# Row sums of two half-heads at once on 32 array columns, a later normalising multiply, and earlier loads, in a fused attention and gMLP block

## The chip, the cores and the metric

The kernel runs on one core of one Trainium2 chip. The metric is the device time of one execution in microseconds (us). Before: median 1973.52 us of 4 runs (1971.62 to 1976.08).

## The reference, cut to what matters

```python
h = _layernorm(x) * (1 + ca) + sa
x = x + ga * _A_ref(h, A_k_cache, A_v_cache, A_wq, A_wo)   # attention, 32 heads of 128, 2048 tokens
h = _layernorm(x) * (1 + cb) + sb
x = x + gb * _B_ref(h, B_w_in, B_w_sp, B_b_sp, B_w_out)    # gMLP, not touched by the change

# in _A_ref:
scores = einsum('bhqd,bhkd->bhqk', q, k_cache) * Dh ** -0.5
p = softmax(scores)                      # needs the sum of exp(scores) over the 2048 keys
o = einsum('bhqk,bhkd->bhqd', p, v_cache)
return o.transpose(...).reshape(B, Sq, H * Dh) @ wo
```

## The kernel before

Attention works in 64 half-heads `i` (32 heads, 1024 queries each) of 16 steps `kb` (128 keys each). A step makes scores (`sps`, two matmuls), takes the exponential on ScalarE (`pt`), multiplies by V (`ops`, two matmuls), and adds `pt` to a running sum `pacc` on VectorE. Queries of a later half (`qps`, 16 matmuls a half) are filled in between by the table `FILL`. At the end of a half, VectorE copies the two `ops` banks to `ou`.

`pacc` still has to be summed over its 128 partitions, inverted, and spread over all partitions:

```python
def bank_ps(...):  return psum.tile(..., tag="bank", bufs=3)   # two ops banks a half, three in all
def side_ps(...):  return psum.tile(..., tag="side", bufs=1)   # shared by qps and dps

def finish_den(i):
    dps = side_ps("dps", [P, 8])
    pv = state[i]["pacc"][:].rearrange("p (q c) -> p c q", c=8)
    for c_ in range(8):                      # weights: 128 columns of pacc; moving: ONE column of ones
        nc.tensor.matmul(dps[:, c_:c_ + 1], pv[:, c_, :], ones_bf[:, 0:1], start=True, stop=True)
    rec = small.tile([P, 8], FP32)
    nc.vector.reciprocal(out=rec[:], in_=dps[:])
    nc.sync.dma_start(rec_dram[i]..., rec[:])                  # 4 KB out
    rbc = att.tile([P, 1024], FP32, bufs=2)
    nc.sync.dma_start(rbc[:], rec_dram[i].partition_broadcast(P))   # 0.5 MB back, to all partitions
    state[i]["rbc"] = rbc

def normalise(i):
    oT = att.tile([P, 1024], BF16, bufs=2)
    nc.vector.tensor_mul(out=oT[:], in0=state[i]["ou"][:], in1=state[i]["rbc"][:])
    nc.sync.dma_start(oT_dram[h, :, ...], oT[:])
# ...
for g, (i, kb) in enumerate(steps):
    # ... exp, scores two steps ahead, fill, ops, pacc, ou ...
    if kb == 6 and i > 0:     finish_den(i - 1)
    elif kb == 12 and i > 0:  normalise(i - 1)

load_slab(0, outw)                     # oT of all heads for 256 tokens
attend_out(0, range(5)); finish_den(2 * H - 1); attend_out(0, range(5, H - 1)); normalise(2 * H - 1)
# ... then load_slab(1), load_slab(2), and for each tile ti of 128 tokens:
    xt = mid.tile([P, D], BF16, bufs=2); nc.sync.dma_start(xt[:], x_dram[:, ti, :])   # x_in
    attend_out(ti, ...)                # 64 acc matmuls
    # x1 = acc * ga + xt, layer norm -> hb; the next tile's TensorE work transposes hb (hps)
```

The softmax here doesn't subtract the row's maximum and nothing guards it: scores larger than these inputs give would overflow.

## Time and profile before

| | before |
|---|---|
| median | 1973.52 us |
| span of the profiled run | 1969.8 us |
| one half-head (from one `dps` to the next) | 17.99 us |
| its 80 matmuls of 512 columns, 0.2158 us each | 17.26 us |
| its 8 `dps` matmuls | 0.51 us |
| left over | about 0.2 us |

The page calls the TensorE (PE) 97% busy. The ends of pipelined matmuls are modelled there, so that share says little about what is lost; the chain of waits says more. It goes back from the last instruction to whatever released each step. Here is its summary by line for the middle of attention, 110 to 1240 us, in the kernel before:

```profile
by line: PE ops L279 39.2%; PE sps L209 38.4%; PE qps L190 19.1%; PE dps L233 2.8%; issue 0.2%; DVE pacc L289 0.1%; DVE oT L248 0.1%; DVE ou L285 0.1%; DVEq L289 0.0%; DVE qT L194 0.0%
```

`ops` and `sps` have the same number of matmuls of the same shape, and yet `ops` has 0.8% more of the chain, 9 us. The chain in order of time shows where they are (kernel before; columns: start in us, length in us, what):

```profile
604.32 0.43 PE qps L190 x2
604.75 0.22 PE ops L279
604.97 0.03 issue
605.00 0.38 PE ops L279
605.37 0.43 PE sps L209 x2
...
611.63 0.51 PE dps L233 x8
...
629.62 0.52 PE dps L233 x8
```

Two matmuls in a row take 0.43 us. At the start of a half the second `ops` takes 0.03 + 0.38 in place of 0.22: it had to be released, and in the records it starts 0.41 us after the matmul before it in place of 0.22. That is 0.19 us, once a half. What released it is on VectorE (DVE), in the timeline of the kernel before (start in us, length, instruction, idle time before it in brackets):

```profile
601.12 0.69 DVE L194 CAST qT<-qps 128x512 bf16<-128x512 f32 x1 [1.27 <-PE qps L190]
601.73 1.22 DVE L248 TENSOR_TENSOR oT<-ou,rbc 128x1024 bf16<-128x1024 f32 x1
602.86 1.48 DVE L289 TENSOR_TENSOR pacc<-pacc,pt 128x1024 bf16<-128x1024 bf16 x2
604.26 0.68 DVE L285 COPY ou<-ops 128x512 f32<-128x512 f32 x1
```

The `ou` copy frees the bank and ends at 604.94, just ahead of the matmul at 605.00. This is no accident of one half: the records have 61 such late `ops` matmuls, each 52 to 54 ns after the end of an `ou` copy. The copy is late because the multiply `oT` runs just before it. Finally, the waits at the transition from attention to the next stage (kernel before, 1235 to 1300 us; columns: total us, times, longest us):

```profile
DVE x L358 <- DMA x_in<-in_A_x_dram: 10.3, 1, 10.3
...
PE hps L144 <- DVE hb L139: 3.6, 1, 3.6
```

The load of `x_in` is queued behind 4 MB of slabs, VectorE waits for it, and the TensorE then stands 3.6 us.

### The profile page before, as it was taken

How to read it: one execution, taken by the hardware profiler on the slowest of the kernel's cores; microseconds unless marked ns; L12 is line 12 of the kernel's file. 1: busy time of each engine (PE TensorE's matmuls, PEld its weight loads, DVE VectorE, ACT ScalarE, POOL GpSimd, SP SyncE). 2: the span in 40 equal slices, each digit the busy share in tenths (PEclk: the TensorE clock that was granted, in tenths of full speed). 3: DMA queues.
4: the chain of work that ended last, by engine and by line, in shares of the span. 5: the costliest groups of instructions: out<-in, count | busy, mean ns of one | idle time of the engine just before them, and what ended most of it. 6: DMA issues, size and time to landing. Idle time of an engine off the chain costs nothing.

```text
span 1969.8 us, 24541 instructions
## 1 busy us (share of the span) xinstructions
PE 1905.1 (97%) x9313; PEld 886.1 (45%) x9313; DVE 1223.4 (62%) x1969; ACT 1105.7 (56%) x1149; POOL 27.0 (1%) x54
## 2 busy tenths in 40 slices
PE   5399999999999999999999999999999999999999
PEld 2244444444444444444444444444445544444444
DVE  4977777777777777777777777454446500233334
ACT  0089889898988898889888988300003333000000
POOL 0100000000000000000000000000000000000000
PEclk9599999999999999999999999999999999999999
DMA  9313222323323324234334322645215010223102
GB/s 318 87 42 88 77 80 81 92 70 86 82 70 90 89 60 109 70 112 124 106 93 127 88 78 58 167 136 171 82 43 124 1 32 22 75 49 91 37 7 75
DMA packets 279399, 171.74 MB, mean 87 GB/s; under 512 B 193648, under 2 KB 245872, under 8 KB 279280
## 3 DMA queue, kind: packets, MB, share of 16 engines
q1 hardware_dynamic: 279280, 170.16, 31.4%
q8 instruction: 73, 1.20, 0.3%
q14 instruction: 46, 0.38, 0.1%
HBM read 120.06 MB, written 24.90 MB: 74 GB/s over the span
## 4 chain that ended last, share of the span: by engine, by line
PE 94%; DMA 2%; DVE 2%; SPq 1%; POOL 0%; issue 0%; ACT 0%; POOLq 0%; DVEq 0%
PE ops L279 23%; PE sps L209 22%; PE qps L190 11%; PE acc L322 10%; PE gps L425 10%; PE zps L375 5%; PE bo L446 5%; PE zps L409 5%; PE dps L233 2%; DMA wm<-in_w_mod_dram 1%; SPq L308 1%; DMA xt<-in_A_x_dram 1%; PE mod_ps L110 1%; DVE stats L134 1%; PE hps L144 0%; DVE h1T L145 0%
## 5 line engine op out<-in xcount | busy, mean ns | idle before, releaser
L268 ACT ACTIVATE pt<-sps 128x1024 bf16<-128x1024 f32 x1024 | 1033.1, 1024 | 211.0 <-PE sps L209 179.7
L289 DVE TENSOR_TENSOR pacc<-pacc,pt 128x1024 bf16<-128x1024 bf16 x896 | 615.7, 687 | 125.8 <-ACT pt L268 78.4
L279 PE MATMUL ops<-pt,v_sb 128*128 128x512 bf16 x2048 | 618.8, 379 | 2.7 <-DVE ou L285 0.6
L209 PE MATMUL sps<-qT,kT 128*128 128x512 bf16 x2048 | 608.7, 379 | 0.8 <-DVE qT L194 0.6
L190 PE MATMUL qps<-h1T,wq_t 128*128 128x512 bf16 x1024 | 357.6, 382 | 3.4 <-DVE qT L194 2.2
L279 PEld LDWEIGHTS <-v_sb 128*128 128x128 bf16 x2048 | 199.9, 98 | 242.6 <-issue 0.8
L209 PEld LDWEIGHTS <-kT 128*128 128x128 bf16 x2048 | 197.4, 98 | 240.7 <-issue 22.3
L322 PE MATMUL acc<-wo_t,ot 128*128 128x512 bf16 x992 | 216.9, 379 | 0.3 <-DMA ot<-oT_dram 0.3
L377 ACT ACTIVATE z<-zps 128x448 bf16<-128x448 f32 x64 | 34.8, 544 | 294.8 <-PE zps L375 291.9
L425 PE MATMUL gps<-wsp,z 128*128 128x512 bf16 x896 | 193.9, 379 | 0.0
L428 DVE TENSOR_TENSOR g<-gps,b_bc 128x512 bf16<-128x512 f32 x56 | 38.8, 692 | 222.1 <-PE gps L425 222.1
L194 DVE CAST qT<-qps 128x512 bf16<-128x512 f32 x128 | 88.5, 691 | 135.4 <-PE qps L190 135.4
L190 PEld LDWEIGHTS <-wq_t 128*128 128x128 bf16 x1024 | 100.8, 99 | 125.4 <-issue 6.4
L322 PEld LDWEIGHTS <-ot 128*128 128x128 bf16 x992 | 96.3, 98 | 114.1 <-DMA ot<-oT_dram 0.8
L425 PEld LDWEIGHTS <-z 128*128 128x128 bf16 x896 | 87.7, 98 | 105.7
L375 PE MATMUL zps<-z2w,h2T 128*128 128x448 bf16 x512 | 97.3, 352 | 0.0
L446 PE MATMUL bo<-w_out_t,z1T 128*128 128x512 bf16 x448 | 97.2, 379 | 0.0
L409 PE MATMUL zps<-h2T,z1w 128*128 128x512 bf16 x448 | 96.9, 379 | 0.0
L248 DVE TENSOR_TENSOR oT<-ou,rbc 128x1024 bf16<-128x1024 f32 x62 | 75.4, 1215 | 0.0
L375 PEld LDWEIGHTS <-h2T 128*128 128x128 bf16 x512 | 50.0, 98 | 46.5 <-issue 0.2
L411 ACT ACTIVATE z1T<-zps 128x512 bf16<-128x512 f32 x56 | 33.4, 597 | 63.3 <-PE zps L409 63.3
L446 PEld LDWEIGHTS <-z1T 128*128 128x128 bf16 x448 | 43.9, 98 | 52.8
(59 smaller groups left out, 708.9 us busy)
## 6 DMA issues: line engine op xcount, KB each, us to landing
rbc<-rec_dram SPq DMA_DIRECT2D x64, 512.0 KB, 3.6
v_sb<-in_A_v_cache_dram SPq DMA_DIRECT2D x32, 512.0 KB, 4.7
oT_dram<-oT SPq DMA_DIRECT2D x62, 256.0 KB, 2.3
wm<-in_w_mod_dram SPq DMA_DIRECT2D x12, 1024.0 KB, 7.1
ot<-oT_dram SPq DMA_DIRECT2D x24, 512.0 KB, 6.7
wq_t<-in_A_wq_dram SPq DMA_DIRECT2D x8, 1024.0 KB, 8.3
wo_t<-in_A_wo_dram SPq DMA_DIRECT2D x8, 1024.0 KB, 5.7
xt<-in_A_x_dram SPq DMA_DIRECT2D x16, 256.0 KB, 2.7
```

What stands on the lines that cost most here:

```text
L190: nc.tensor.matmul(box["ps"][:], wq_t[:, dc, hc:hc + DH], h1T[:, dc, q0:q0 + 512], start=(dc == 0), stop=(dc == KD - 1))
L194: nc.vector.tensor_copy(out=out_t[:, j * 512:(j + 1) * 512], in_=box["ps"][:])
L209: nc.tensor.matmul(sps[:, j * 512:(j + 1) * 512], kts[h][:, kb * P:(kb + 1) * P], qts[(h, qh)][:, j * 512:(j + 1) * 512], start=True, stop ...
L248: nc.vector.tensor_mul(out=oT[:], in0=state[i]["ou"][:], in1=state[i]["rbc"][:])
L268: nc.scalar.activation(pt[:], s_tiles.pop(g)[:], ACT.Exp, scale=SCALE)
L279: nc.tensor.matmul(o_ps[j][:], vs[h][:, kb, :], pt[:, j * 512:(j + 1) * 512], start=(kb == 0), stop=(kb == NKB - 1))
L289: nc.vector.tensor_add(out=pacc[:], in0=pacc[:], in1=pt[:])
L322: nc.tensor.matmul(accs[ti][:, sl], lhs, wo_t[:, hh, sl], start=(hh == 0), stop=(hh == H - 1))
L375: nc.tensor.matmul(zps[:], h2T[:, dc, ti * P:(ti + 1) * P], z2w[:, dc, sl], start=(dc == 0), stop=(dc == KD - 1))
L409: nc.tensor.matmul(zps[:], w[:, dc, :], h2T[:, dc, q * 512:(q + 1) * 512], start=(dc == 0), stop=(dc == KD - 1))
L425: nc.tensor.matmul(gps[:], z2[s][:, f * P:(f + 1) * P], wsps[q][:, s, :], start=(s == 0), stop=(s == NT - 1))
L446: nc.tensor.matmul(bo[:], z1T[:, f, ti * P:(ti + 1) * P], w_out_t[:, f, sl], start=(f == 0), stop=(f == NF - 1))
```

## The change

Its intent: fewer and better shaped row-sum matmuls (a stationary block of 32 columns of ones, `pacc` moving, four groups of 32 array columns, two half-heads at once); the multiply at a place where VectorE is not needed for `ou`; loads at the transition ahead of need.

```diff
-    ones_bf = consts.tile([P, 1], BF16)
+    ones_bf = consts.tile([P, 32], BF16)
@@ def finish_den(i):
-        dps = side_ps("dps", [P, 8])
-        ... eight matmuls of one moving column, reciprocal, one write, one broadcast load (above)
+        # row sums of steps i and i + 1 at once
+        dps = side_ps("dps", [P, 512])
+        for k in range(2):
+            pacc = state[i + k]["pacc"]
+            for b in range(4):
+                nc.tensor.matmul(dps[32 * b:32 * b + 32, 256 * k:256 * k + 256],
+                                 ones_bf[:, :], pacc[:, 256 * b:256 * b + 256],
+                                 start=True, stop=True)
+        den = att.tile([P, 16, 32], FP32, name="den", tag="den")
+        nc.vector.transpose(den[:].rearrange("p c r -> p (c r)"), dps[:])
+        rec = small.tile([P, 32], FP32, name="rec", tag="rec")
+        nc.vector.memset(rec[:], 0.0)
+        nc.vector.reciprocal(out=rec[:, 0:16], in_=den[:, :, 0])
+        turned = small.tile([P, 32], FP32, name="turned", tag="turned")
+        nc.vector.transpose(turned[:], rec[:])
+        for b in range(4):
+            nc.sync.dma_start(rec_dram[i:i + 2]...[b], turned[32 * b:32 * b + 16, :])
+        rbc = att.tile([P, 2, 1024], FP32, name="rbc", tag="rbc", bufs=1)
+        nc.sync.dma_start(rbc[:], rec_dram[i:i + 2].partition_broadcast(P))
+        ... each of the two halves gets its part of rbc
@@ buffers: oT 2 -> 1, pacc 2 -> 3, ou 2 -> 3; load_slab and attend_out defined before the loop
+        if i == len(halves) - 1 and kb == 4:
+            load_slab(0, outw)
@@ in the loop
-        if kb == 6 and i > 0:
-            finish_den(i - 1)
-        elif kb == 12 and i > 0:
-            normalise(i - 1)
+        if kb == 6 and i > 0 and i % 2 == 0:
+            finish_den(i - 2)
+        elif kb == 3 and i > 2:
+            normalise(i - 3)
+        elif kb == 9 and i == len(halves) - 1:
+            normalise(i - 2)
@@ after the loop
-    finish_den(2 * H - 1)
+    finish_den(2 * H - 2)
     attend_out(0, range(5, H - 1))
+    normalise(2 * H - 2)
     normalise(2 * H - 1)
@@ next stage: x_in with 3 buffers, two tiles ahead, the first two issued before the slabs
+    load_x(0)
+    load_x(1)
     load_slab(1, mid)
...
-        xt = mid.tile([P, D], BF16, name="x_in", tag="x_in", bufs=2)
-        nc.sync.dma_start(xt[:], x_dram[:, ti, :])
+        if ti + 2 < NT:
+            load_x(ti + 2)
```

## The prediction

> **What bounds it now.** The TensorE. In the chain of waits, from 110 to 1240 us (attention), 39.2% are the `ops` matmuls, 38.4% `sps`, 19.1% `qps`, 2.8% `dps`. One half-head repeats every 17.99 us (`dps` to `dps`, 611.63 to 629.62). Its 80 matmuls of 512 columns at 0.2158 us (0.43 for two in the chain) need 17.26. The remaining 0.73 us is 0.51 us of eight `dps` matmuls (row sums, 64 ns each for one moving column) and about 0.2 us once a half: at 604.97 the chain has 0.03 us of issue and then one `ops` matmul of 0.38 instead of 0.22. The timeline shows why: this second `ops` bank becomes free with the `ou` copy, VectorE 604.26 to 604.94. VectorE was late because `oT` (1.22 us) ran at 601.73, just before the half ends.
>
> **What the change does, per pair of halves.**
> - Row sums: 16 single-column matmuls (2 x 0.51 = 1.02 us, all on the chain) become 8 of 256 columns, each on 32 array columns. One after another they would take 8 x 0.108 = 0.86 us (estimate from 0.2158 for 512) plus switching. The Trainium skill, "TensorEngine Tiling (Array Packing)", Key Properties, says that different tiles run matmuls in parallel and that changing the mode drains the TensorE; no trace yet shows either. If four run together, two rounds take about 0.22 us; with weight loads and two drains I estimate 0.6 us for the eight. Saved: 0.4 us a pair.
> - VectorE: 2 x 0.21 us of reciprocals become two transposes, a memset and a reciprocal, about 1.1 us (the large one estimated at 0.69 like the 512-element f32 copies). VectorE has room. But the side bank now stays taken until the large transpose ends; the next `qps` matmul uses it 0.86 us later (the four matmuls in between). That is nearly a tie; I allow 0.15 us a pair of new wait.
> - `oT` moves from step 12 to step 3. The `ou` copy can then start when the last `ops` ends, and the 0.2 us a half should go: 64 x 0.19 = 12 us. At step 3 VectorE has 0.88 us idle before the next cast, so 1.13 us more fits nearly.
> - Transition: `x_in` and the first slab load earlier. Now VectorE waits 10.27 us for `x_in` behind the slab loads and TensorE stands 3.6 us (waits: PE `hps` for `hb`). This goes. Against it, the tail chain of the last row sums grows (about 1.4 us on VectorE instead of 0.2, four writes, 1 MB broadcast instead of 0.5) to about 11.5 us, and 52 `acc` matmuls (11.2 us) cover it: perhaps 0.5 to 1 us of wait.
>
> **Sum.** 32 x (0.42 - 0.15) = 8.6; plus 12; plus 3.6 - 0.8: about 23 us. Stages before 100 us and after 1300 us do not change. Predicted 1950 us, 8 in 10 from 1935 to 1965. Faster by over 2%: 0.09; within 2%: 0.90; slower: 0.01.
>
> **What would show it.** The half-head period: from 17.99 us to a pair of about 35.3 (2 x 17.26 + 0.75). No 0.38 us `ops` piece at a half's start. The `dps` piece of a pair: 0.6 us if tiles run together, 1.0 or more if not. `qps` waiting for VectorE's `den` after row sums: 0 to 0.15 us. No `x_in` wait near the transition.
>
> **What would make it wrong.** Column tiles that run one after another with expensive drains (then about 10 us gain only); a 32-bit transpose at half speed, which would stall `qps` by 0.6 us a pair; tiles so cheap (0.3 us) that the gain nears 35 us; a slow tail.

## The result, and the profile after

| | before | after |
|---|---|---|
| median | 1973.41 us (13 runs) | 1936.74 us (8 runs, 1935.81 to 1936.99) |
| ratio | | 0.9812, 95% interval 0.9803 to 0.9822 |
| span of the profiled run | 1969.8 us | 1935.0 us |
| two half-heads | 35.98 us | 34.98 us |

A ratio is the mean time of one kernel's fast runs over that of the other's fast runs of the same rounds, so it is not quite the ratio of the medians. The gain is 36.7 us, 1.9%. It lies inside the range predicted, close to its lower end; the mean forecast was 23 us.

The chain of waits of the kernel after, by line, for the middle of attention (110 to 1200 us):

```profile
by line: PE sps L209 39.8%; PE ops L314 39.5%; PE qps L190 19.8%; PE dps L234 0.9%
```

`ops` no longer exceeds `sps`, and the row sums fell from 2.8% to 0.9%. In order of time, with the `dps` of the next pair (kernel after, chain):

```profile
592.01 0.43 PE qps L190 x2
592.45 0.43 PE ops L314 x2
592.88 0.43 PE sps L209 x2
...
598.71 0.43 PE ops L314 x2
599.14 0.33 PE dps L234 x8
599.47 0.54 PE sps L209 x2
600.01 0.43 PE ops L314 x2
600.44 0.23 PE qps L190
...
634.12 0.33 PE dps L234 x8
```

At the start of the half (592.45) two `ops` take 0.43 us: the 0.38 piece is gone. All eight `dps` matmuls take 0.33 us, and the `sps` pair behind them 0.54, which is 0.11 more than any other pair. So a pair of halves pays 0.44 us for its row sums. Before it paid 0.51 twice, and 0.02 twice in an `sps` pair of 0.45 behind them: 1.06 us. VectorE of the kernel after, timeline:

```profile
589.42 1.48 DVE L324 TENSOR_TENSOR pacc<-pacc,pt 128x1024 bf16<-128x1024 bf16 x2
591.40 0.69 DVE L320 COPY ou<-ops 128x512 f32<-128x512 f32 x1 [0.50 <-PE ops L314]
...
595.40 1.22 DVE L259 TENSOR_TENSOR oT<-ou,rbc 128x1024 bf16<-128x1024 f32 x1
596.54 1.48 DVE L324 TENSOR_TENSOR pacc<-pacc,pt 128x1024 bf16<-128x1024 bf16 x2
598.31 0.69 DVE L194 CAST qT<-qps 128x512 bf16<-128x512 f32 x1 [0.29 <-PE qps L190]
598.92 0.68 DVE L324 TENSOR_TENSOR pacc<-pacc,pt 128x1024 bf16<-128x1024 bf16 x1
599.52 0.72 DVE L238 STREAM_TRANSPOSE den<-dps 128x512 f32<-128x512 f32 x1
```

The `ou` copy now waits for the TensorE (0.50 us idle before it) and no longer the other way round. The `oT` multiply at step 3 still leaves 0.29 us before the cast. The transpose ends about 600.24. The `qps` matmul that wants its bank comes right after it, as the timeline of the TensorE shows (kernel after; the chain lays its pieces end to end, so its 600.44 is not the time at which this matmul started):

```profile
599.84 0.59 PE L314 MATMUL ops<-pt,v_sb 128*128 128x512 bf16 x2
600.29 0.38 PE L190 MATMUL qps<-h1T,wq_t 128*128 128x512 bf16 x1
```

In the records this `qps` starts 52 to 53 ns after the end of the transpose in every pair of the loop, the same distance as between the `ou` copy and the `ops` matmul above. So it is released by the transpose. It starts about 232 ns after the matmul before it, where 216 are usual: a wait of 0.016 us a pair. At the transition (1200 to 1265 us) no wait for `x_in` and no `hps` wait is left in the list of waits, and the chain there is TensorE work with only one gap, 1.2 us for the last exponential. The table of the period accounts for the gain: 1.00 us a pair, 32 pairs, 32 us; the transition gives about 4. (The two profiled spans differ by 34.8 us and not by 36.7: the profiled run of before was the fastest of its 13.)

### The profile page after: what moved, and what is told of

The parts are those of the page before. It is cut to its first block, busy times and chain, and to the rows that moved or that the text cites. A ratio compares the mean times of both kernels' runs of the same rounds, so it can differ in the third digit from the quotient of the medians.

```text
span 1935.0 us, 24004 instructions
## 1 busy us (share of the span) xinstructions
PE 1876.4 (97%) x9057; PEld 856.5 (44%) x9057; DVE 1251.3 (65%) x2033; ACT 1102.1 (57%) x1149; POOL 27.0 (1%) x54
## 4 chain that ended last, share of the span: by engine, by line
PE 96%; DVE 2%; DMA 2%; POOL 0%; ACT 0%; issue 0%; SPq 0%; POOLq 0%
PE sps L209 23%; PE ops L314 23%; PE qps L190 12%; PE acc L285 11%; PE gps L448 10%; PE zps L398 5%; PE bo L469 5%; PE zps L432 5%; DMA wm<-in_w_mod_dram 1%; DMA xt<-in_A_x_dram 1%; PE mod_ps L110 1%; PE dps L234 1%; PE hps L144 0%; DVE stats L134 0%; DVE h1T L145 0%; DVE h L138 0%
## 5 line engine op out<-in xcount | busy, mean ns | idle before, releaser
L314 PE MATMUL ops<-pt,v_sb 128*128 128x512 bf16 x2048 | 609.0, 379 | 0.3 <-ACT pt L303 0.3
L400 ACT ACTIVATE z<-zps 128x448 bf16<-128x448 f32 x64 | 34.8, 544 | 290.5 <-PE zps L398 287.6
L145 DVE COPY h2T<-hps 128x1024 bf16<-128x1024 bf16 x16 | 11.1, 691 | 98.7 <-PE hps L144 98.7
```

The source lines that it names most:

```text
L314: nc.tensor.matmul(o_ps[j][:], vs[h][:, kb, :], pt[:, j * 512:(j + 1) * 512], start=(kb == 0), stop=(kb == NKB - 1))
```

## The experiments

Each ran with five rounds. "More than after" means against 1936.7 us, the median of after both times it was timed (1936.74 and 1936.71). Medians of before in the three sets of rounds were 1974.94, 1973.99 and 1975.98 us.

### 1. `move_only`: the kernel before, with only the multiply moved

```diff
-            ou = att.tile([P, 1024], FP32, name="ou", tag="ou", bufs=2)
+            ou = att.tile([P, 1024], FP32, name="ou", tag="ou", bufs=3)
...
-        elif kb == 12 and i > 0:
+        elif kb == 3 and i > 1:
+            normalise(i - 2)
+        elif kb == 12 and i == len(halves) - 1:
             normalise(i - 1)
```

> The kernel before, with only the normalising multiply moved from step 12 of the next half to step 3 of the half after that (one more buffer for its input). Theory: the gain has three parts that add up, and this is one: the ou copy is no longer late, the 0.38 us ops piece at each start of a half turns into 0.22, so 64 x 0.19 = 12 us less, about 1961 us, and the half-head period in the trace falls from 17.99 to about 17.78 us. Rival: VectorE is only 62% busy and not the bottleneck, so moving its work gives nothing (1973 us) and the whole gain of the change is TensorE work taken away.

Measured: 1963.05 us against 1974.94, ratio 0.9941 (0.9929 to 0.9954), so 11.9 us less. The period in the chain is 17.80 us (606.88 to 624.68). The theory's 12 us hold; the rival, by which an engine at 62% cannot matter, falls. An average says nothing about who is late at one instant of each half.

### 2. `early_only`: the kernel before, with only the early loads

```diff
+        if i == len(halves) - 1 and kb == 4:
+            load_slab(0, outw)
...
+    load_x(0)
+    load_x(1)
     load_slab(1, mid)
...
-        xt = mid.tile(..., bufs=2); nc.sync.dma_start(xt[:], x_dram[:, ti, :])
+        if ti + 2 < NT:
+            load_x(ti + 2)
```

> The kernel before, with only the loads at the transition moved earlier: the first slab inside the last half, x_in two tiles ahead and in front of the slabs. Theory: the 3.6 us wait of hps for hb and the 0.35 us wait for the first slab go, 3 to 4 us less, about 1969.5 us. Rival: the slabs are then later and a new wait of the same size appears among the acc matmuls (no change, 1973 us).

Measured: 1968.98 us, ratio 0.9972 (0.9960 to 0.9985), which is 3 to 8 us less than before (6.0 by the medians). The profiled spans differ by 3.0 us (1966.8 against 1969.8). No new wait appeared.

### 3. `old_sums`: the kernel after, with single-column row sums

```diff
-        dps = side_ps("dps", [P, 512]) ... (eight matmuls, transpose, memset, reciprocal, transpose, four writes)
+        dps = side_ps("dps", [P, 16])
+        for k in range(2):
+            pv = state[i + k]["pacc"][:].rearrange("p (q c) -> p c q", c=8)
+            for c_ in range(8):
+                nc.tensor.matmul(dps[:, 8 * k + c_:8 * k + c_ + 1], pv[:, c_, :],
+                                 ones_bf[:, 0:1], start=True, stop=True)
+        rec = small.tile([P, 2, 8], FP32, name="rec", tag="rec")
+        nc.vector.reciprocal(out=rec[:]..., in_=dps[:])
+        nc.sync.dma_start(rec_dram[i:i + 2]..., rec[:])
```

> The kernel after, with the row sums made by 16 single-column matmuls for the two halves again, nothing else changed. Theory: each pair pays 1.02 us again instead of the 0.44 us that the chain after shows (0.33 dps, 0.11 longer sps), so 32 x 0.58 = 18.6 us more than after, about 1955 us. Rival (the whole gain is the row sums): back to about 1970 us.

Measured: 1955.45 us, 18.7 us more than after. Its chain has 1.00 us for sixteen `dps`. The matmuls alone are worth half of the gain, and not all of it.

### 4. `late_norm`: the kernel after, with the multiply at step 12 again

```diff
-        elif kb == 3 and i > 2:
-            normalise(i - 3)
-        elif kb == 9 and i == len(halves) - 1:
+        elif kb == 12 and i > 1:
             normalise(i - 2)
```

> The kernel after, with the normalising multiply back at step 12, everything else kept. Theory: the ou copy is late again, the second ops matmul of a half takes 0.38 us in the chain, 64 x 0.19 = 12 us more than after, about 1949 us. Rival: no change against after (1937 us).

Measured: 2027.69 us (one run of four at 2034.95), 91 us more than after and 53 us more than before. Both expectations missed by far. The list of waits of `late_norm` names it (total us, times, longest us):

```profile
PE ops L314 <- DVE ou L320: 70.0, 31, 3.7
DVE oT L259 <- DMA rbc<-rec_dram: 65.2, 31, 3.6
```

Both happen 31 times, once a pair. The chain of `late_norm` in one pair:

```profile
598.81 0.64 DVE den L238
...
601.94 1.62 DMA rec_dram<-turned
...
603.71 4.55 DMA rbc<-rec_dram
...
608.36 0.06 DVE oT L259
608.42 1.08 issue
609.50 0.69 DVE pacc L324
...
610.98 0.61 DVE ou L320
611.59 0.04 issue
611.64 0.38 PE ops L314
```

For two halves at once, the way from the row sums to the broadcast is long: 0.72 us for the large transpose (before: one reciprocal of 0.21), four writes issued one after another, and a load of 1 MB that took 4.55 us here where the load of 0.5 MB took 3.6 before. It is 9.5 us from 598.73, the start of `den`, to the landing at 608.26. Step 12 comes sooner than that. In the timeline of `late_norm` VectorE stands idle for 1.92 us in front of `oT` and does the `pacc` additions and the `ou` copy, which come behind it in the program, only after it; the TensorE waits for the bank (the 70.0 us above).

### 5. `half_late`: one of the two multiplies at step 12, with its data there

```diff
-        elif kb == 3 and i > 2:
+        elif kb == (12 if i % 2 and i < len(halves) - 1 else 3) and i > 2:
             normalise(i - 3)
```

> The kernel after, with the normalising multiply of every even half moved from step 3 to step 12 of the same later half, so that its broadcast has long landed; the other half's stays at step 3. late_norm lost 91 us, where 12 were forecast, because the multiply at step 12 stood waiting for the 1 MB broadcast and VectorE with it. Theory: with the data there, only the late ou copy remains: 31 halves x 0.19 = 6 us more than after (about 1943 us), and a 0.38 us ops piece at the start of every second half. Rival: the step-12 place is bad by itself, then some 40 us more (about 1978 us).

Measured: 1942.05 us, 5.3 us more than after. The expectation counted 31 halves; the edit moves 30 (odd `i` from 3 to 61), and the records have exactly 30 late `ops` matmuls, each 54 to 55 ns after the end of an `ou` copy. The chain shows the late piece in every second half only, 35.18 us apart:

```profile
594.27 0.03 issue
594.30 0.38 PE ops L314
600.94 0.33 PE dps L234 x8
629.45 0.03 issue
629.48 0.38 PE ops L314
```

So step 12 costs 0.18 us by its place (5.3 over 30), some 11 us if both halves of each pair pay it. The other 80 us of `late_norm` are left for the data not being there, which is how its list of waits has it (70.0 us of TensorE waits behind `ou`, 65.2 us of VectorE waits for `rbc`).

### 6. `one_group`: all eight row-sum matmuls on the same 32 array columns

```diff
-                nc.tensor.matmul(dps[32 * b:32 * b + 32, 256 * k:256 * k + 256],
+                nc.tensor.matmul(dps[0:32, 256 * k:256 * k + 256],
...
-        nc.vector.transpose(den[:]..., dps[:])
+        nc.vector.transpose(den[0:32]..., dps[0:32, :])        # den is set to 1 once
```

> The kernel after, with all eight row-sum matmuls of a pair sent to the same 32 array columns (the result is wrong on purpose; the unwritten part of den is set once). Theory: the 0.33 us of after comes from four column groups working at once; in one group the eight run one after another, 8 x 0.108 = 0.86 us, so 32 x 0.53 = 17 us more than after, about 1954 us. Rival: 256-column matmuls with 32 columns of weights are cheap by themselves: no change, 1937 us.

Measured: 1956.91 us, 20.2 us more than after. (Its output is wrong, which doesn't matter for the time. The comparison with the reference still passed, so a passed comparison is weak evidence for the row sums here.) The chain of `one_group`:

```profile
607.40 0.98 PE dps L237 x8
608.38 0.54 PE sps L209 x2
```

The records put the starts of the eight matmuls 109 to 120 ns apart (1, 120, 230, 339, 448, 557, 666, 775). In the kernel after they start at 1, 5, 8, 11 and again at 120, 125, 128, 130 ns: four at a time, in two rounds. That the groups work together is shown. The expectation was 17 us because it counted 0.86 us of streaming against all of the 0.33. In both kernels the next `sps` weight load starts 201 ns after the last row-sum start, so only the first 0.13 us of the 0.33 grew, to 0.78: 0.65 x 32 = 20.8 us.

### 7. `group_by_group`: the two loops exchanged

```diff
-        for k in range(2):
-            pacc = state[i + k]["pacc"]
-            for b in range(4):
+        for b in range(4):
+            for k in range(2):
+                pacc = state[i + k]["pacc"]
```

> The kernel after, with the two loops of the row sums exchanged: both matmuls of one column group in a row, then the next group. Result right. Theory: matmuls start in program order, so the second of a group holds up the next group; five rounds of 0.107 us instead of two, about 0.65 us instead of 0.33, and 32 x 0.32 = 10 us more than after, about 1947 us. Rival: groups are queued independently and the order does not matter: 1937 us.

Measured: 1937.61 us, 0.9 us more than after. The theory fell. In the chain the eight take 0.34 us. In the records they start at 2, 9, 15, 22 and then at 122, 129, 135, 142 ns. In program order the second matmul belongs to the same group as the first, and `one_group` shows that such a pair starts 109 ns apart or more. Four starts within 20 ns can therefore only be in four different groups: later groups went ahead of the waiting second matmul of the first. The spacing says the same: these starts are 6 to 7 ns apart, where in the kernel after, which changes the group with every matmul, they are 3 to 4 ns apart. This is inferred from the times; the records do not name the group. The extra 0.9 us is small and the two ranges do not overlap in the rounds of `after` (1937.42 to 1937.71 against 1935.81 to 1936.99), but they do in those of `after_again` (up to 1937.61); the chain has 0.01 us more in `dps` and 0.01 more in the `qps` behind it. The Trainium skill, "TensorE: Matmul & The Clock Gate", Part 3, "The mechanism", says that matmuls are "strict FIFO, no reordering". By this measurement that does not hold across column groups.

### 8. `four_wide`: four matmuls of 512 columns for eight of 256

```diff
-            for b in range(4):
-                nc.tensor.matmul(dps[32 * b:32 * b + 32, 256 * k:256 * k + 256],
-                                 ones_bf[:, :], pacc[:, 256 * b:256 * b + 256],
+            for j in range(2):
+                b = 2 * k + j
+                nc.tensor.matmul(dps[32 * b:32 * b + 32, :],
+                                 ones_bf[:, :], pacc[:, 512 * j:512 * j + 512],
```

> The kernel after, with four row-sum matmuls of 512 columns per pair in place of eight of 256, each column group still streaming 512 columns. Result right. Theory: 0.22 us of streaming and a fixed cost of switching on either side stay, so the two chain pieces together stay near 0.44 us; 0 to 2 us less than after, about 1936 us. Rival: the cost goes with the number of matmuls and weight loads, 0.055 us each: 0.22 us less a pair, 7 us less, about 1930 us.

Measured: 1936.13 us (1935.56 to 1936.84), 0.6 us less than after, and the two ranges overlap. The chain has 0.33 and 0.54 us, the same as after. The cost does not go with the number of matmuls and weight loads. This version is simpler, but it is not shown to be faster.

### 9. `after_again`: the kernel after, for the rounds of the next two

> The kernel after once more, on the same chip as the next two, to have its ratio in the same rounds: 1936 to 1938 us.

Measured: 1936.71 us, ratio 0.9804 (0.9790 to 0.9817). Against 0.9812 above, this shows how well two sets of rounds agree.

### 10. `no_early`: the kernel after, without the early loads

```diff
-        if i == len(halves) - 1 and kb == 4:
-            load_slab(0, outw)
+    load_slab(0, outw)                       # after the loop
...
-    load_x(0)
-    load_x(1)
...
-        if ti + 2 < NT:
-            load_x(ti + 2)
+        xt = mid.tile(..., bufs=2); nc.sync.dma_start(xt[:], x_dram[:, ti, :])
```

> The kernel after, with the loads at the transition put back to where they were before (first slab after the last half, x_in behind the slabs, two buffers). Theory: parts add up, so the wait of hps for hb returns, 3.5 to 5.5 us more than after (about 1941 us). Rival: the parts overlap and taking one away costs less than 1.5 us.

Measured: 1949.10 us, 12.4 us more than after: a miss, where the same loads give 3 to 8 us in `early_only`. The timeline of `no_early` (TensorE lines, idle time in brackets):

```profile
1219.67 3.91 PE L285 MATMUL acc<-wo_t,ot 128*128 128x512 bf16 x10 [1.49 <-DMA ot<-oT_dram]
...
1256.48 1.04 PE L144 MATMUL hps<-identity,hb 128*128 128x128 bf16 x8 [6.94 <-DVE hb L139]
1257.31 15.48 PE L285 MATMUL acc<-wo_t,ot 128*128 128x512 bf16 x62
```

and its busy time, granted clock and DMA share by stretch (the number before the DMA share is the clock):

```profile
1218.00:1222.00 4.00, 2.52 (x8) 0.92 (x8) 2.31 (x4) 1.04 (x2) 0.00 (x0) 0.78 1.19 305
1222.00:1226.00 4.00, 4.00 (x22) 1.44 (x21) 1.23 (x4) 0.00 (x0) 0.00 (x0) 0.79 0.51 123
...
1256.00:1260.00 4.00, 3.52 (x15) 1.87 (x16) 2.83 (x5) 0.00 (x0) 0.00 (x0) 0.50 0.01 2
```

The tail of the last pair is longer than that of one half, so the slabs start later and `x_in` behind them later still; the `hps` wait is 6.94 us where it was 3.6. In addition the clock fell. The 0.78 and 0.79 are means: the trace's record of the clock has 0.50 from 1220.25 for 3.41 us, and again from 1254.38 for 6.83 us, and 1.00 between. The ten `acc` matmuls after the first wait took 3.91 us where after needs 2.3 (1.6 us lost), and the `hps` and `acc` pieces after the second took 1.04 + 15.71 us in the chain where after has 0.45 + 13.81 (2.5 us lost). With the two waits, 1.49 and 6.94, this makes 12.5 us, about the 12.9 by which the profiled spans differ. The Trainium skill, "TensorE: Matmul & The Clock Gate", Part 1, says that the clock halves after an idle window of about 3.4 us, which is free-running. The wait of 6.94 us agrees. So does the 3.6 us wait in the kernel before, after which the clock stayed at 1.00: counted in steps of 3.413 us from the last change of the clock in that trace (97.82), a window ends at 1278.83, in the middle of the wait (1277.1 to 1280.7), so that neither window was idle throughout. The fall at 1220.25 does not agree: in the 3.41 us before it the TensorE was idle for 1.8 us only (waits of 0.32 and 1.49), much as in those two windows of the kernel before (1.7 and 1.9 us).

### 11. `extra_visit`: one more visit to the 32-column mode

```diff
+        if kb == 13 and i > 0 and i % 2 == 0:
+            idle = side_ps("idle", [P, 64])
+            for b in range(4):
+                nc.tensor.matmul(idle[32 * b:32 * b + 32, :], ones_bf[:, :],
+                                 h1T[:, 0, 0:64], start=True, stop=True)
```

> The kernel after, with one more visit of the TensorE to the 32-column mode in every second half, at step 13: four matmuls of 64 columns whose result nobody reads. Theory: of the 0.44 us a pair of after, 0.22 is streaming and about 0.2 is a fixed cost of going into the mode and out of it (0.09 us in front, 0.1 us behind), so each visit costs about 0.22 us, 31 x 0.22 = 7 us more than after. Rival: there is no fixed cost and the four small matmuls cost their streaming alone, 0.03 us, so 1 us more.

Measured: 1944.37 us, 7.7 us more than after, so 0.25 us for each of the 31 visits. Its chain:

```profile
610.78 0.14 PE idle L343 x4
610.92 0.54 PE sps L209 x2
```

0.14 plus the 0.11 of the longer `sps` pair is 0.25 us for 64 columns of streaming, which alone would be 0.03 us. So a visit has a fixed cost of about 0.22 us, and the rival falls. The Trainium skill, "TensorEngine Tiling (Array Packing)", Key Properties, says that a change of tiling mode drains the TensorE; this run fits that and gives the size of a whole visit. That the drain makes up all of the fixed 0.22 us is not shown.

No run beat after by more than the spread of its runs. The one that came nearest is `four_wide`.

## Why the prediction was right or wrong

**Right: what bounds the kernel, and the `ou` copy.** The prediction read 0.19 us a half from the chain and named the multiply as its cause; it forecast 12 us. `move_only` gave 11.9 us, and `half_late`, which puts back about half of it, cost 5.3. The 0.38 us piece went, as said. The multiply fitted at step 3: 0.29 us stayed idle before the cast.

**Right in kind, mis-sized: the row sums.** "with weight loads and two drains I estimate 0.6 us for the eight. Saved: 0.4 us a pair." They cost 0.33 + 0.11 = 0.44 us, and what they replaced cost 1.06, so 0.62 us a pair was saved: 20 us over 32 pairs where 13 were forecast. `old_sums` puts it at 18.7. Both halves of the estimate were right in kind. `one_group` shows that four groups run together, and `extra_visit` and `four_wide` show that the rest is a fixed cost of the visit. Only the size of that fixed cost, 0.22 us, was below what I allowed (0.38, the 0.6 less 0.22 of streaming). The prediction had named this case under what would make it wrong: "tiles so cheap (0.3 us) that the gain nears 35 us".

**Right in kind, mis-sized: the new wait for the side bank.** "That is nearly a tie; I allow 0.15 us a pair of new wait." It is a tie: the transpose releases the `qps` matmul in every pair, but the wait is 0.016 us, 0.5 us in all. The estimate put 0.86 us between the row sums and that `qps`; in the chain it is 0.97 (0.54 + 0.43). This term was 4.3 us too much (32 x 0.134). There is no slack left: in `group_by_group` the `qps` follows the transpose by the same 53 to 54 ns, and comes about 248 ns after the matmul before it in place of 232.

**Slightly wrong: the tail.** "perhaps 0.5 to 1 us of wait". The weight load waited 0.2 us and no gap shows in the chain. The transition gave the whole 4 us.

Put together, 20 + 12 + 4 less 0.5 is about 35.5 us, and 36.7 were measured. The forecast of 23 was short by the row sums (7) and the waits that did not come (4.3 and 0.8). All these errors went the same way, so none made up for another, and the time lies only 1.7 us inside the range predicted: the mechanisms were right, the sizes cautious.

**Not seen at all: the parts depend on each other.** The prediction treated the moved multiply as a separate gain. `late_norm` shows that batching two halves without it is 53 us slower than before, because the broadcast arrives 9.5 us after the row sums. And the early loads, worth 3 to 8 us alone, are worth 12.4 once the tail is that of a pair, 4.1 of them through the clock. The sum came out because the change contained all three. The losses that would follow from leaving one out were not in the estimate; and the prediction's remark that the tail chain grows was not carried through to the loads that queue behind it.

What stays open: why the clock fell after waits of 0.32 and 1.49 us in `no_early`; and whether row sums of four halves in one visit would save another half of the 0.22 us, which was not built.

## What to carry to other kernels

Look in the chain for single pieces that are longer than their neighbours of the same shape: an engine that is idle a third of the time can still be late at one instant of each loop, and moving its work away from that instant cost nothing measurable here. Reductions over partitions with ones as the narrow stationary operand can run in four column groups at once, whatever the order in which they are written, but each visit to the narrow mode has a fixed price (0.22 us here), so make few visits. Batching lengthens the latency of what it batches: move the consumer back by at least that much in the same edit, and check the last iteration, where nothing is left to hide it.

## What the Trainium skill lacked or had wrong

- "TensorEngine Tiling (Array Packing)", Key Properties, names the drain on a change of tiling mode without a size. Here a visit to the 128x32 mode and back costs 0.25 us with 64 moving columns, about 0.22 us of it fixed (`extra_visit`); how much of that is the drain was not separated.
- "TensorE: Matmul & The Clock Gate", Part 3, calls matmuls strict FIFO. With two matmuls of each column group in a row, four of the eight still started within 20 ns and the block took 0.34 us instead of 0.33 (`group_by_group`); matmuls of the same group start 109 to 120 ns apart (`one_group`). Across column groups the order is not kept, as inferred from these times.
- The same page, Part 1, gives about 3.4 us as the idle window after which the clock halves. In `no_early` the clock was 0.50 for 3.41 us from 1220.25 on, though the TensorE had been idle for only 1.8 of the 3.41 us before (waits of 0.32 and 1.49); ten matmuls took 3.91 us where 2.3 is usual. Windows of the kernel before with 1.7 and 1.9 us of idle time left the clock at 1.00, so the runs give no other rule.
- "VectorE: DVE Perf Modes", The three transpose paths, has a time for VectorE's transpose only in bf16 (311 ns for 128x128). In 32 bits out of PSUM, 128x512 took 717 ns, and 128x32 from SBUF 213 ns.
